# A second space for transposed tokens, DMA transposes spread over two stages, and W2's second half in pieces

## The chip, the cores and the metric

One core of one Trainium2 chip (trn2). The metric is the device time of one execution in microseconds (us), where lower is better. A profile is one execution taken by the hardware profiler; its span is some 1.8 us shorter than the timed run. The median of the kernel before moved by 3 us between sessions, so kernels of different sessions are best compared by their ratio to it.

## The reference, cut to what matters

```python
x = A_x                                                    # 2048 tokens x 1024, bf16
x = x + spectral(layernorm(x))                             # 2-D FFT filter, "layer A"
x = x + mish(layernorm(x) @ w1 + b1) @ w2                  # F = 3584, "layer B", dense
x = x + spectral(layernorm(x))
x = x + mish(layernorm(x) @ w1 + b1) @ w2
```

Only layer B is touched. It occurs twice ("layer one" and "layer two" below).

## The kernel before: what the change and the argument touch

The 2048 tokens are 16 tiles of 128 (`j`), or four chunks of 512 (`c`). A pair of chunks goes through the first matmul together: a Strassen-Winograd scheme takes seven block products of 4 matmuls each instead of eight. It needs sums of blocks of the tokens (made by VectorE) and sums of blocks of the weights (made by GpSimd in layer one, stored, and loaded ready-made in layer two). A "step" below is one pass of `quads`: 28 matmuls, 6.05 us. "Direct products" are those of the first matmul without the scheme.

```python
def fill_slot(self, b, fg):                 # weights of one step into one slot
    r = self.r_w1d[fg]
    if r.writes:                            # layer two: raw weights and sums come from DRAM
        self.dma(self.sp, b.ap, self.w1s_d[fg], ...)
        return
    self.load_w1(b.raw, fg, [b.res])        # 512 KB, sync queue
    for dst, x, y, op in (...):             # four sums on GpSimd
        self.op(self.pool, lambda e, ...: e.tensor_tensor(dst, x, y, op), reads=[b.res], writes=[b.rs])
    self.dma(self.pool, self.w1s_d[fg], b.ap, ...)          # stored for later, 896 KB

def turned(c, t, xn):                       # a tile transposed by eight DMAs, all on the sync queue
    x = XT[c % 2]                           # chunks 2 and 3 reuse the space of chunks 0 and 1
    for db in range(8):
        self.dma(sp, x.ap[:, db, t*P:(t+1)*P], xn.ap[:, db*P:(db+1)*P], ..., transpose=True)

# layer B, second half of the first pair, cut
early = self.open_slots("WE", self.ob["W2"], 3)
for n in range(3):
    self.fill_slot(early[n], 6 + n)
...                                         # direct first matmul of chunk 1, residual additions
ws = self.open_slots("WS", self.ob["WS"], 3)
for n in range(3):
    self.fill_slot(ws[n], 9 + n)
order = early + [ws[n % 3] for n in range(5)]
def after(n):                               # called when step n's products are issued
    if n in (3, 4):
        self.fill_slot(order[n + 3], 9 + n)
    if 2 <= n < 6:
        for i in range(2*n - 4, min(2*n - 2, 7)): load_w2(0, i)
quads(list(range(6, 14)), order, open_pair(), after)        # first block stage: 8 steps
...
for t in range(8): self.stats_dve(8 + t)                    # tiles 8 to 15, only now
self.scales(8, 8)
for n in range(16):                                         # second matmul of the first pair
    if n < 8:
        turned(2 + n // 4, n % 4, self.apply(8 + n))        # normalise and transpose
    mm2(n % 8 // 4, n % 4, n // 8)
    if n == 12: B = open_pair()                             # token sums of the second pair
quads(list(range(14)), order, B, after)                     # second block stage: 14 steps
```

A buffer allocated over another inherits all its readers and writers, so whoever is recorded as a reader of a tile makes the next writer of that space wait.

## Time and profile before

| | before |
|---|---|
| median of the runs beside the change | 1019.0 us (1016.8 to 1020.0) |
| profiled span, granted TensorE clock | 1014.7 us, 0.980 |
| layer one: approach (from the start of a group of 71 or 72 direct products, here at 137.12 us, to the first block product) | 41.44 us |
| layer one: first block stage, second block stage | 50.11, 108.77 us |
| layer two: the same three | 34.97, 49.30, 92.02 us |

The lines behind these numbers are in the prediction below. The kernel is bound by TensorE, so read its timeline: each row is a start, a length, a group of matmuls, and in brackets the hole before it with what ended the hole. Layer two is the same program without GpSimd's weight sums, and so it shows what layer one could be.

### The profile page before, as it was taken

The page shows a single profiled execution, that of the slowest core. Times are in us where ns is not written, and L with a number is a line of the kernel's source. Part 1 is how long each engine was busy: PE and PEld are TensorE (multiplying, and loading weights), DVE is VectorE, ACT ScalarE, POOL GpSimd, SP SyncE. Part 2 cuts the span into 40 slices and gives each one's busy share as a digit, 9 for nine tenths or more (in the row PEclk, how much of TensorE's full clock was granted, in tenths as well). Part 3 has the DMA queues.
Part 4 walks back from the last instruction along what each step waited for, and adds up shares of the span by engine and source line. Part 5 has one row for each costly group of instructions (what it writes and reads, how often), then busy time and mean ns, then how long its engine had stood idle before and what let it go on. Part 6 is the DMA issues. An engine that isn't in the chain of part 4 may idle for free. (4 is left out here: it accounts for less than half of the span.)

```text
span 1014.7 us, 13594 instructions
## 1 busy us (share of the span) xinstructions
PE 925.4 (91%) x5572; PEld 489.6 (48%) x5650; DVE 508.5 (50%) x915; ACT 377.6 (37%) x531; POOL 156.5 (15%) x184
## 2 busy tenths in 40 slices
PE   1799789999998499999998987999999989999998
PEld 0576565444443144444446765754444434444443
DVE  6797576558341655524335865655731145551111
ACT  7798473550000055510007975745300015550000
POOL 4831035342300060000431200000000000000000
PEclk9999899999999599999999998999999999999999
DMA  9969833467321054340751796233551124424000
GB/s 284 288 190 323 215 102 141 145 218 238 109 58 46 34 207 148 107 171 29 202 115 27 222 224 174 110 109 123 193 176 26 25 96 149 160 91 145 32 27 25
DMA packets 143598, 139.62 MB, mean 138 GB/s; under 512 B 74464, under 2 KB 124464, under 8 KB 143536
## 3 DMA queue, kind: packets, MB, share of 16 engines
q1 hardware_dynamic: 130432, 98.41, 32.6%
q0 software_dynamic: 10928, 38.69, 11.7%
q10 hardware_dynamic: 2176, 1.66, 0.5%
q8 instruction: 44, 0.72, 0.3%
q14 instruction: 18, 0.15, 0.0%
HBM read 100.64 MB, written 33.55 MB: 132 GB/s over the span
## 5 line engine op out<-in xcount | busy, mean ns | idle before, releaser
L1228 PE MATMUL PS<-ARENA 128*128 128x512 bf16 x1756 | 385.6, 379 | 1.9
L1177 PE MATMUL PS<-ARENA 128*128 128x512 f16 (+1 forms) x1210 | 274.1, 386 | 26.6 <-DVE ARENA L1156 12.6
L1228 PEld LDWEIGHTS PS<-ARENA 128*128 128x128 bf16 x1792 | 175.2, 98 | 211.8 <-DVE ARENA L1182 0.8
L1182 DVE TENSOR_TENSOR ARENA<-PS,ARENA 128x512 f32<-128x512 f32 x220 | 152.2, 692 | 116.7 <-PE PS L1177 115.1
L1177 PEld LDWEIGHTS PS<-ARENA 128*128 128x128 bf16 x1232 | 121.1, 99 | 178.9 <-DVE ARENA L1182 16.3
L1240 DVE TENSOR_TENSOR XS<-PS,XS 128x512 bf16<-128x512 f32 x63 | 43.3, 690 | 228.5 <-PE PS L1228 228.5
L577 ACT ACTIVATE ARENA<-PS 128x512 f32<-128x512 f32 (+2 forms) x66 | 51.8, 785 | 257.2 <-PE PS L1177 246.3
L1187 ACT ACTIVATE ARENA<-ARENA,B 128x512 bf16<-128x512 f32 x132 | 95.2, 721 | 61.4 <-DVE ARENA L1182 55.2
L1141 PE MATMUL PS<-ARENA 128*128 128x256 bf16 (+1 forms) x570 | 88.0, 311 | 0.4
L1084 POOL TENSOR_TENSOR ARENA<-ARENA 128x512 bf16<-128x512 bf16 x56 | 66.6, 1189 | 119.6 <-DMA ARENA<-in_B_w_dram 95.0
L1141 PEld LDWEIGHTS PS<-ARENA 128*128 128x128 bf16 x576 | 55.8, 99 | 27.7 <-issue 2.1
L469 DVE BATCH_NORM_STATS2 BN<-XS 128x6 f32<-128x512 bf16 x99 | 63.8, 673 | 5.3 <-DMA XS<-in_A_x_dram 4.3
L1145 ACT ACTIVATE ARENA<-PS,B 128x256 bf16<-128x256 f32 (+1 forms) x72 | 38.4, 542 | 41.8 <-PE PS L1141 41.2
L1156 DVE TENSOR_TENSOR ARENA<-ARENA 128x2048 f16<-128x2048 bf16 x16 | 19.8, 1238 | 60.0 <-DMA ARENA<-ARENA 41.3
L1187 ACT ACTIVATE ARENA<-PS,B 128x512 bf16<-128x512 f32 x44 | 30.3, 688 | 36.2 <-PE PS L1177 36.2
L441 ACT ACTIVATE RS<-MV,EPS 128x2 f32<-128x2 f32 (+2 forms) x5 | 1.5, 298 | 95.7 <-DVE MV L472 83.7
L802 PE MATMUL PS<-ARENA 128*128 128x256 bf16 x256 | 32.4, 273 | 3.8 <-DVE ARENA L791 3.2
L780 ACT ACTIVATE ARENA<-PS 128x1024 bf16<-128x1024 f32 x32 | 33.3, 1071 | 4.5 <-PE PS L776 4.5
L728 PE MATMUL PS<-FD,ARENA 128*128 128x256 bf16 (+1 forms) x256 | 31.8, 271 | 2.5 <-DVE ARENA L995 1.3
L784 DVE TENSOR_TENSOR ARENA<-ARENA 128x1024 bf16<-128x1024 bf16 x32 | 22.0, 689 | 19.8 <-ACT ARENA L780 14.2
L813 ACT ACTIVATE ARENA<-PS 128x1024 bf16<-128x1024 f32 x28 | 29.9, 1090 | 3.7 <-PE PS L802 3.7
L1023 PE MATMUL PS<-MT,ARENA 128*128 128x32 bf16 (+1 forms) x512 | 21.7, 200 | 10.3 <-DMA ARENA<-u_scratch 7.0
(95 smaller groups left out, 695.6 us busy)
## 6 DMA issues: line engine op xcount, KB each, us to landing
ARENA<-in_B_w_dram SPq DMA_DIRECT2D x68, 512.0 KB, 6.5
ARENA<-w1s_scratch SPq DMA_DIRECT2D x30, 896.0 KB, 4.6
w1s_scratch<-ARENA POOLq DMA_DIRECT2D x14, 896.0 KB, 4.3
u_scratch<-ARENA SPq DMA_DIRECT2D x14, 512.0 KB, 3.5
ARENA<-u_scratch SPq DMA_DIRECT2D x14, 512.0 KB, 6.1
w_scratch<-ARENA POOLq DMA_DIRECT2D x8, 512.0 KB, 7.6
ARENA<-w_scratch POOLq DMA_DIRECT2D x8, 512.0 KB, 5.5
out_dram<-XS SPq DMA_DIRECT2D x16, 256.0 KB, 2.0
```

Source lines behind the costliest of these rows:

```text
L469: self.op(self.dve, lambda e: e.bn_stats(self.BN[:, j, 6 * h:6 * h + 6], self.XS[:, j, 512 * h:512 * h + 512]), reads=[self.r_xs[j]], part ...
L577: fn = (lambda e: e.activation(dst, src, ACT.Copy)) if scale is None else \
L780: self.op(act, lambda e: e.activation(x.ap.rearrange("p a b -> p (a b)"), ps, ACT.Copy, scale=SIG), reads=banks, writes=[x.res])
L802: fns.append(lambda e, c=c, part=part: e.matmul(ps[:, c * 256:(c + 1) * 256], yk.ap[:, part, c * P:(c + 1) * P], t[:, (128, 0)[part]:(384, ...
L1084: self.op(self.pool, lambda e, dst=A(dst), x=A(x), y=A(y), op=op: e.tensor_tensor(dst, x, y, op), reads=[b.res], writes=[b.rs])
L1141: fns.append(lambda e, db=db, bank=bank, fl=fl: e.matmul(PS[:, bank, 0:w], wb.ap[:, db, fl * P:(fl + 1) * P], x.ap[:, db, tok], start=(db ...
L1145: self.op(act, lambda e, bank=bank, ft=ft: e.activation(at.ap[:, ft, tok], PS[:, bank, 0:w], ACT.Mish, bias=self.B1[:, ft:ft + 1]), reads= ...
L1177: self.group([lambda e, db=db: e.matmul(PS[:, bank, :], A[:, db, :], mov[:, db, :], start=(start and db == 0), stop=(db == 3), skip_group_ ...
L1182: self.op(dve, lambda e: e.tensor_tensor(dst.ap, PS[:, bank, :], x.ap, ALU.add), reads=[self.r_bank[bank], x.res], writes=[dst.res])
L1187: self.op(act, lambda e: e.activation(at.ap[:, ft, :], src, ACT.Mish, bias=self.B1[:, ft:ft + 1]), reads=[res, self.r_b1], writes=[ra])
L1228: fns.append(lambda e, i=i, ft=ft: e.matmul(PS[:, bank, :], at.ap[:, ft, t * P:(t + 1) * P], W2[h][ft // 4].ap[:, ft % 4, :], start=(i == ...
L1240: self.op(dve, lambda e: e.tensor_tensor(xs, PS[:, bank, :], xs, ALU.add), reads=[self.r_bank[bank]], writes=[self.r_xs[j]])
```

## The change

The intent: the second pair's transposes should no longer wait for the first pair's products, so that the token sums are there when the second block stage starts. So chunks 2 and 3 get spaces of their own; W2's second half moves into pieces of free space; statistics, normalisation and transposes of tiles 8 to 11 come forward into the first block stage; and GpSimd's first weight sums wait until the eighth tile (`xn[7]`) is normalised. Core of the diff:

```diff
-        self.ob = dict(AT0=0, AT1=36 * K, XT1=28 * K, XT0=120 * K, W2=64 * K, ...
+        self.ob = dict(AT0=0, AT1=36 * K, XT1=28 * K, XT0=120 * K, XT2=104 * K, XT3=112 * K, W2=64 * K, ..., XN2=140 * K,
@@ fill_slot
-    def fill_slot(self, b, fg):
+    def fill_slot(self, b, fg, after=()):
-            self.op(self.pool, ..., reads=[b.res], writes=[b.rs])
+            self.op(self.pool, ..., reads=[b.res] + list(after), writes=[b.rs])
@@ turned: queue closures instead of issuing; turn(n) issues the next n
+        def turn(n):
+            for _ in range(min(n, len(turning))):
+                turning.pop(0)()
@@ load_w2
-            W2[h][i] = self.alloc(f"W2_{h}_{i}", self.ob["W2"] + h * 28672 + i * 4096, [4, 512])
+            off = (28, 32, 120, 124, 92, 96, 100)[i] * 1024 if h else self.ob["W2"] + i * 4096
+            if h and not i and W2[1][0]:
+                off = 104 * 1024
@@ before the first block stage
-            self.fill_slot(early[n], 6 + n)
+            self.fill_slot(early[n], 6 + n, [xn[7].res])
...
+            if fg < 4:
+                for j in range(4 * fg, 4 * fg + 4):
+                    residual(j)
+            if fg == 3:
+                token_sums(0, last=False)
+            if fg == 4:
+                for j in range(8, 12):
+                    self.stats_dve(j)
+        self.scales(8, 4)
+        normal(8)
+        turn(8)
         ws = self.open_slots("WS", self.ob["WS"], 3)
         for n in range(3):
             self.fill_slot(ws[n], 9 + n)
+        B = token_sums(0)
@@ after(n) of the first block stage
+            if n < 3:
+                normal(9 + n)
+            elif n < 7:
+                self.stats_dve(9 + n)
+            turn(4)
@@ second matmul
+            if n == 0:
+                self.scales(12, 4)
+            if n < 4:
+                normal(12 + n)
             mm2(t // 4, t % 4, n // 8)
-            if n == 12:
-                B = open_pair()
+            turn(4)
+            if n == 10:
+                token_sums(1, last=False)
+                B = token_sums(1)
@@ after the second block stage
-        for i in range(7):
+        for i in (0, 4, 5, 6):
             load_w2(1, i)
```

The last lines are a side effect: three pieces of W2's second half stay where they are and aren't loaded again, six loads of 512 KB less in the whole kernel.

More of the change, by code (lines that the diff above doesn't have):

```diff
@@ L369, in layout @@
                       FT=140 * K, BT=144 * K + 512, WT=self.W1_OFF)
-        self.ob = dict(AT0=0, AT1=36 * K, XT1=28 * K, XT0=120 * K, W2=64 * K, JUNK=54 * K, SUMS=92 * K, TS=128 * K,
+        self.ob = dict(AT0=0, AT1=36 * K, XT1=28 * K, XT0=120 * K, XT2=104 * K, XT3=112 * K, W2=64 * K, JUNK=54 * K, SUMS=92 * K, TS=128 * K, XN2=140 * K,
                        WS=self.arena_bytes - 21 * K)
@@ L1083, in fill_slot @@
                               ("S4", "A12", "S2", ALU.subtract)):
-            self.op(self.pool, lambda e, dst=A(dst), x=A(x), y=A(y), op=op: e.tensor_tensor(dst, x, y, op), reads=[b.res],
+            self.op(self.pool, lambda e, dst=A(dst), x=A(x), y=A(y), op=op: e.tensor_tensor(dst, x, y, op), reads=[b.res] + list(after),
                     writes=[b.rs])
@@ L1091, in layer_B, with open_xt @@
         base = 28 * li
-        XT, AT, r_xt, r_at = [None, None], [None, None], [None, None], [None, None]
+        XT, AT, r_xt, r_at = [None] * 4, [None, None], [None] * 4, [None, None]
         nt, nh, no = [0], [0], [0]
+        def open_xt(c):
+            off = self.ob[f"XT{c}"]
+            XT[c] = self.alloc(f"XT{c}", off, [8, 512])
+            r_xt[c] = self.sub_res(XT[c], f"xt{c}h", 2, off, 8192)
+            for r in r_xt[c]:
+                r.begin()
         def transposed(c, t, xn, eng=None):
@@ L1099, in transposed @@
             if t == 0:
-                if XT[c % 2] is None:
-                    off = self.ob[f"XT{c % 2}"]
-                    XT[c % 2] = self.alloc(f"XT{c % 2}", off, [8, 512])
-                    r_xt[c % 2] = self.sub_res(XT[c % 2], f"xt{c % 2}h", 2, off, 8192)
-                for r in r_xt[c % 2]:
-                    r.begin()
+                open_xt(c)
             fns = []
@@ L1110, in transposed, with one @@
             self.group(fns, reads=[xn.res, self.r_ident], writes=[self.r_bank[bank]])
-            dst = XT[c % 2].ap[:, :, t * P:(t + 1) * P]
+            dst = XT[c].ap[:, :, t * P:(t + 1) * P]
             src = PSb[:, bank, :].rearrange("p (a b) -> p a b", b=P)
             fn = (lambda e: e.activation(dst, src, ACT.Copy)) if eng is act else (lambda e: e.tensor_copy(dst, src))
-            self.op(eng or dve, fn, reads=[self.r_bank[bank]], parts=[r_xt[c % 2][t // 2]])
+            self.op(eng or dve, fn, reads=[self.r_bank[bank]], parts=[r_xt[c][t // 2]])
+        turning = []
         def turned(c, t, xn):
-            xn.unread = False
-            x = XT[c % 2]
-            if t == 0:
-                for r in r_xt[c % 2]:
-                    r.begin()
-            for db in range(8):
-                self.dma(sp, x.ap[:, db, t * P:(t + 1) * P], xn.ap[:, db * P:(db + 1) * P], f"xt{c % 2}_{t}", reads=[xn.res],
-                         parts=[r_xt[c % 2][t // 2]], transpose=True)
+            x, r = XT[c], r_xt[c][t // 2]
+            for db in range(8):
+                def one(db=db):
+                    self.dma(sp, x.ap[:, db, t * P:(t + 1) * P], xn.ap[:, db * P:(db + 1) * P], f"xt{c}_{t}", reads=[xn.res],
+                             parts=[r], transpose=True)
+                    if db == 7:
+                        xn.unread = False
+                turning.append(one)
+        def turn(n):
+            for _ in range(min(n, len(turning))):
+                turning.pop(0)()
         def mm1(c, fg, half=None, mid=()):
             wb = self.w1_buf[fg]
-            x = XT[c % 2]
+            x = XT[c]
             tok = slice(0, 512) if half is None else slice(256 * half, 256 * half + 256)
@@ L1142, in mm1 @@
                         PS[:, bank, 0:w], wb.ap[:, db, fl * P:(fl + 1) * P], x.ap[:, db, tok], start=(db == 0), stop=(db == 7)))
-                self.group(fns, reads=[wb.res] + (r_xt[c % 2] if half is None else [r_xt[c % 2][half]]), writes=[self.r_bank[bank]])
+                self.group(fns, reads=[wb.res] + (r_xt[c] if half is None else [r_xt[c][half]]), writes=[self.r_bank[bank]])
                 at, ra = AT[c % 2], r_at[c % 2][ft]
@@ L1147, in mm1, with token_sums @@
                         reads=[self.r_bank[bank], self.r_b1], writes=[ra])
-        def open_pair():
-            T = [self.alloc(f"TS{i}", self.ob["TS"] + 4096 * i, [4, 512], F16) for i in range(3)]
-            lo, hi = [[XT[c].ap[:, 4 * k:4 * k + 4, :] for c in range(2)] for k in range(2)]
+        def token_sums(p, last=True):
+            c0, c1 = 2 * p, 2 * p + 1
+            lo, hi = [[XT[c].ap[:, 4 * k:4 * k + 4, :] for c in (c0, c1)] for k in range(2)]
             t3 = lo[1].bitcast(F16)
-            both = r_xt[0] + r_xt[1]
+            both = r_xt[c0] + r_xt[c1]
             tt = lambda dst, x, y, reads, writes: self.op(
                 dve, lambda e: e.tensor_tensor(dst, x, y, ALU.subtract), reads=reads, writes=writes)
+            if last:
+                tt(t3, hi[1], lo[1], r_xt[c0], r_xt[c1])
+                T = self.T
+                return {"B11": (lo[0], r_xt[c0]), "B21": (hi[0], r_xt[c0]), "B22": (hi[1], r_xt[c1]), "T3": (t3, r_xt[c1]),
+                        "T1": (T[0].ap, [T[0].res]), "T2": (T[1].ap, [T[1].res]), "T4": (T[2].ap, [T[2].res])}
+            self.T = T = [self.alloc(f"TS{i}", self.ob["TS"] + 4096 * i, [4, 512], F16) for i in range(3)]
             tt(T[0].ap, lo[1], lo[0], both, [T[0].res])
@@ L1159, in open_pair @@
             tt(T[2].ap, hi[0], T[1].ap, both + [T[1].res], [T[2].res])
-            tt(t3, hi[1], lo[1], r_xt[0], r_xt[1])
-            return {"B11": (lo[0], r_xt[0]), "B21": (hi[0], r_xt[0]), "B22": (hi[1], r_xt[1]), "T3": (t3, r_xt[1]),
-                    "T1": (T[0].ap, [T[0].res]), "T2": (T[1].ap, [T[1].res]), "T4": (T[2].ap, [T[2].res])}
         def open_sums():
@@ L1227, in mm2 @@
             for i, ft in enumerate(range(NF)):
-                fns.append(lambda e, i=i, ft=ft: e.matmul(
-                    PS[:, bank, :], at.ap[:, ft, t * P:(t + 1) * P], W2[h][ft // 4].ap[:, ft % 4, :],
+                fns.append(lambda e, i=i, ft=ft, w=W2[h][ft // 4]: e.matmul(
+                    PS[:, bank, :], at.ap[:, ft, t * P:(t + 1) * P], w.ap[:, ft % 4, :],
                     start=(i == 0), stop=(i == NF - 1 and not summed)))
@@ L1258, in load_w2 @@
         def load_w2(h, i):
-            W2[h][i] = self.alloc(f"W2_{h}_{i}", self.ob["W2"] + h * 28672 + i * 4096, [4, 512])
+            off = (28, 32, 120, 124, 92, 96, 100)[i] * 1024 if h else self.ob["W2"] + i * 4096
+            if h and not i and W2[1][0]:
+                off = 104 * 1024
+            W2[h][i] = self.alloc(f"W2_{h}_{i}", off, [4, 512])
             self.dma(sp, W2[h][i].ap, w2v[:, 4 * i:4 * i + 4, h * 512:(h + 1) * 512], f"w2_{h}_{i}", writes=[W2[h][i].res])
@@ L1346, in layer_B, with normal @@
             mm1(1, fg, 1)
+        def normal(j):
+            if j % 4 == 0:
+                open_xt(j // 4)
+            turned(j // 4, j % 4, self.apply(j))
         for fg in range(2, 6):
             mm1(1, fg)
-            for j in (2 * fg + 4, 2 * fg + 5):
-                residual(j)
+            if fg < 4:
[6 more added lines that the diff above has]
+                    self.stats_dve(j)
+        self.xn_buf = self.xn_out + [self.alloc(f"XN{i}", self.ob["XN2"] + i * 2048, [self.D]) for i in range(2)]
+        self.scales(8, 4)
+        normal(8)
+        turn(8)
         ws = self.open_slots("WS", self.ob["WS"], 3)
@@ L1361, in after @@
                     load_w2(0, i)
-        quads(list(range(6, 14)), order, open_pair(), after)
+            if n < 3:
[3 more added lines that the diff above has]
+            turn(4)
+        quads(list(range(6, 14)), order, B, after)
         for i in range(7):
@@ L1367, in layer_B @@
             self.fill_slot(order[n], n)
-        self.xn_buf = [self.alloc(f"XN{i}", self.ob["TS"] + i * 2048, [self.D]) for i in range(6)]
-        for t in range(8):
-            self.stats_dve(8 + t)
-        self.scales(8, 8)
+        self.xn_buf = [self.alloc(f"XN{i}", self.ob["TS"] + i * 2048, [self.D]) for i in range(4)]
         for n in range(16):
-            if n < 8:
-                b = self.apply(8 + n)
-                turned(2 + n // 4, n % 4, b)
+            if n == 0:
+                self.scales(12, 4)
+            if n < 4:
+                normal(12 + n)
             t = n % 8
             mm2(t // 4, t % 4, n // 8)
-            if n == 12:
-                B = open_pair()
+            turn(4)
+            if n == 10:
+                token_sums(1, last=False)
+                B = token_sums(1)
+        assert not turning
         def after(n):
```

## The prediction

> **What bounds the kernel now.** I read the page first (busy shares, the forty slices), then the waits of TensorE, then the timeline of TensorE, VectorE and the sync queue around each wait, then one table of windows. The kernel has two spectral layers and two dense layers; only the dense ones (from about 120 and from about 620 us) are touched.
>
> ```profile
> PE 925.4 (91%) x5572; PEld 489.6 (48%) x5650; DVE 508.5 (50%) x915; ACT 377.6 (37%) x531; POOL 156.5 (15%) x184
> PE   1799789999998499999998987999999989999998
> PEclk9999899999999599999999998999999999999999
> ...
> PE PS L1177 <- DVE ARENA L1156: 12.6, 2, 8.8
> PE PS L1177 <- DVE ARENA L1182: 11.8, 6, 8.1
> PE PS L1108 <- DVE ARENA L521: 5.2, 5, 3.4
> ```
>
> TensorE is busy 91% of the span, so only its holes matter. The fourteenth slice (330 to 355 us) falls to 4 tenths and its clock to 5 tenths: that is the hole in which the first dense layer waits for the token sums (L1156) of its second chunk pair. The waits list (total, times, longest) puts 12.6 us on those sums over both layers and 11.8 us on additions (L1182) that queue behind other VectorE work. The timeline shows the chain:
>
> ```profile
> 325.36 1.03 PE L1177 MATMUL PS<-ARENA 128*128 128x512 bf16 x4
> 335.15 5.30 PE L1177 MATMUL PS<-ARENA 128*128 128x512 f16 x12 [8.77 <-DVE ARENA L1156]
> 348.55 15.84 PE L1177 MATMUL PS<-ARENA 128*128 128x512 f16 x59 [8.09 <-DVE ARENA L1182]
> ...
> 332.61 5.00 DVE L1156 TENSOR_TENSOR ARENA<-ARENA 128x2048 f16<-128x2048 bf16 x4 [21.66 <-DMA ARENA<-ARENA]
> ...
> 243.73 87.67 SPq L250 DMA_TRANSPOSE ARENA<-ARENA  x64
> ```
>
> The 64 DMA transposes leave one queue one after the other (median 1.23 us each in the rows of that line, 1.37 with stalls), from 243.7 to 331.4 us. They start late because they write over the first pair's tokens, so they must wait for the first block products. The second products are due at 325.4, the sums start at 332.6 and take 5.0 us, and three tiles' worth of postponed residual and normalisation work then holds the adds until 348.6. In the second layer the same stretch has holes of 3.87 and 0.59 us.
>
> The table of windows compares the same work in both layers: approach to the first block products, first products, second products. Columns: window, its length, busy time of PE, PEld, DVE, ACT, POOL, clock, DMA share.
>
> ```profile
> 137.12:178.56 41.44, 36.96 (x242) 22.41 (x243) 29.50 (x48) 19.43 (x35) 24.39 (x23) 0.96 0.46 152
> 641.62:676.59 34.97, 34.75 (x242) 22.06 (x242) 21.25 (x48) 19.43 (x35) 0.00 (x0) 1.00 0.42 153
> 178.56:228.67 50.11, 48.48 (x222) 21.73 (x224) 28.41 (x40) 26.68 (x39) 18.77 (x18) 1.00 0.53 179
> 676.59:725.89 49.30, 48.30 (x221) 21.83 (x224) 28.17 (x40) 26.79 (x39) 0.00 (x0) 1.00 0.34 116
> 325.36:434.13 108.77, 90.44 (x386) 39.04 (x392) 61.88 (x103) 46.45 (x69) 17.15 (x18) 0.91 0.33 117
> 822.59:914.61 92.02, 86.41 (x386) 38.32 (x392) 54.35 (x76) 46.77 (x69) 0.00 (x0) 0.98 0.38 134
> ```
>
> First row against second: equal matmuls, but 6.47 us longer in layer one, where GpSimd works 24.39 us beside VectorE and in layer two not at all.
>
> **What the Trainium skill says.** "TensorE: Matmul & The Clock Gate", the part on the HAM clock gate: after an idle window of some 3.4 us the array runs at half clock until it has been busy again. The trace agrees: after the 8.77 us hole 12 matmuls took 5.30 us (0.44 each, against 0.216), after the 8.09 us hole 59 took 15.84, some 3.1 us too long. "SBUF — State Buffer", section "Who interferes with whom": VectorE and GpSimd share a port pair under an exclusive lock; VectorE copies and tensor_scalar in 2-port modes, and anything with two SBUF inputs, can be blocked by a GpSimd operation. The trace agrees: the normalisation (L521) takes 0.55 us alone and up to 1.28 beside GpSimd. "DMA: Bandwidth & Descriptors", section "Issuing engines are not separate DMA queues": the sequencer's issue time is usually small beside the transfer. Here it is not: 1.23 us of queue per transpose against 2.4 us to landing, so the queue is the resource to count.
>
> **The change, part by part.** (1) Tokens 8 to 15 get a space of their own (XT2, XT3), W2's second half moves into pieces of dead space. Half the transposes now go out during the first block products: 8 before them, 4 after each of the first six; the other 32 in the first eight groups of the second matmul. Those 32 take 32 x 1.23 = 39.4 us, starting once the queue has pushed the weight loads (some 14 us into the stage, as now), so they end about 54 us into a stage of 96.8 us; the sums are placed after the eleventh group, at 66.5. Hence the L1156 wait goes in both layers. Layer two's second stretch: 92.02 - 3.87 - 0.59 - 1.7 (12 cold matmuls, 4.33 - 12 x 0.216) = 85.9. Layer one should reach the same plus some 1.0 for the last tile's chain on VectorE (0.69 + 0.69 + 0.21 + six small operations + 0.55, 3.4 us, ahead of the first add): 86.9 against 108.77. **Gain 21.9 + 6.1.**
>
> (2) GpSimd's first twelve weight sums (16.4 us from first to last, 141.4 to 157.8) now wait for the eighth tile's normalisation. That frees VectorE where TensorE waited 3.38 and 0.67 us plus cold matmuls: layer one's approach should become layer two's 34.97. **Gain 6.5**, quads starting at about 172.1.
>
> (3) The price, in layer one. GpSimd now starts at 152.6 (layer two's time of that normalisation, 657.06, minus the offset of 504.5) and ends at 152.6 + 16.4 + about 2 of blocking = 171. VectorE meanwhile has eight residual additions (4.90 us alone, some 0.75 more each beside GpSimd) and the first token sum, to about 167. The second sum's space covers the buffer of the eighth normalised tile, which the GpSimd sums now count as reading, so it should wait for the last of them: 171.2. Then two sums 2.5, four tiles' statistics 5.53, scales 1.6, one normalisation 0.55, last sum 1.25, one add 0.69: 183.4. TensorE needs sum and add at the fifth product, 172.1 + 16 x 0.216 = 175.6. **Loss 7.8 plus some 3 of cold clock.**
>
> (4) The queue. Eight transposes (9.9 us) stand ahead of three weight loads: 181.4 + 9.9 + 0.4 issue + 3.8 to landing (as at 164.9 to 168.7 now) + 4.9 of GpSimd = 200.4. Step four of the delayed products needs them at 172.1 + 18.2 + 10.8 = 201.1: just hidden. Later steps carry at most 4 x 1.23 + 1.4 us of queue per 6.05 us step; I add **0.6 of loss** for the seventh slot, which already stands 0.63 us now. Layer two has no GpSimd sums: its normalisation ends near 675.5, before the products, loads land near 690 and are needed at 694.7, so nothing is lost.
>
> Sum: 21.9 + 6.1 + 6.5 - 7.8 - 3 - 0.6 = 23.1; 1019.6 - 23.1 = **996.5 us**, which I round to 996.
>
> **Rivals.** (A) Part 3 is avoided: the sums don't collide, or VectorE is ahead of the products as in layer two. For it: layer two's timeline leaves the last sum where TensorE wants it. Against: layer one's GpSimd work merely moves onto VectorE's busiest stretch. Then the loss is only the load path of part 4, some 2 us with the start at 172.6, and the time about 987. (B) Contention is worse, or transposes in the queue delay weight loads in steps 4 to 8: each transposed batch then takes over 6.05 us (1.37 each plus loads is already 6.9), slots come late by several us and the clock falls again: 1002 to 1005. (C) The sums at the eleventh group find transposes unfinished, so the wait merely moves: against it the 12 us of slack; it would give back 5 to 10 us, about 1003. (D) The transfers were hidden anyway: the waits list speaks against it, 8.8 and 8.1 us of it on TensorE's own path.
>
> **Range and chances.** The gains are firm (sizes known from the other layer); the loss in layer one is an estimate from four contended operations, 2 to 14 us. So 987 to 1005. The 2% line is 999.2, some 3 us above the figure: faster 0.70, same 0.29, slower 0.01.
>
> **What would show it.** Right: no wait of L1177 on L1156 near the second products, transposes in two groups, one ending before the second matmul and one half-way through it, the approach window near 35 us with no L1108 wait of 3 us. Part 3 right: a TensorE hole of 5 to 11 us within the first step of layer one's block products, released by VectorE, and the second token sum starting when GpSimd's twelfth sum ends. Part 4: that layer's fourth step free of a wait on GpSimd longer than 2 us. Wrong: a first block stage in layer one of 50 us (then rival A) or over 65 us, or a wait on transposes left in either layer.

## The result, and the profile after

The changed kernel took **1006.3 us** (median of four runs, 1005.8 to 1006.7) against 1019.0 before. The ratio is 0.9878, interval 0.9860 to 0.9895: 1.2% faster. I had said 996, and 1005 as the upper end of the range. (A ratio is the mean time of one kernel's runs over that of the other's runs of the same rounds, so it isn't quite the ratio of the medians quoted.)

First the page of the changed kernel, with the busy share and the clock in 40 slices of 25.1 us. The fourteenth slice, 4 tenths before, is full now. But the eighth to tenth (176 to 251 us) have fallen to 6, 7 and 8 tenths, and the clock there to 7, 9 and 8.

```profile
PE 928.6 (92%) x5650; PEld 490.0 (49%) x5650; DVE 509.1 (51%) x931; ACT 377.6 (38%) x531; POOL 157.7 (16%) x184
PE   1799699678999999999998997999999999999998
PEclk9999799798999999999999998999999999999999
```

Next TensorE's timeline in layer one, from the first block product on:

```profile
173.76 3.87 PE L1188 MATMUL PS<-ARENA 128*128 128x512 bf16 x16
185.66 15.21 PE L1188 MATMUL PS<-ARENA 128*128 128x512 f16 x60 [8.02 <-DVE ARENA L1193]
204.22 19.66 PE L1188 MATMUL PS<-ARENA 128*128 128x512 bf16 x84 [3.35 <-POOL ARENA L1084]
228.40 15.16 PE L1188 MATMUL PS<-ARENA 128*128 128x512 bf16 x56 [4.53 <-POOL ARENA L1084]
...
342.77 3.62 PE L1188 MATMUL PS<-ARENA 128*128 128x512 bf16 x16
347.16 13.12 PE L1188 MATMUL PS<-ARENA 128*128 128x512 f16 x60 [0.77 <-DVE ARENA L1193]
```

The holes at the second block stage (8.77 and 8.09 us) are gone; 0.77 is left. But the first block stage, which had only one of 0.63 us, now has three: 8.02 us in its first step, 3.35 before its fourth, 4.53 before its seventh. The same windows as before (length; busy time of PE, PEld, DVE, ACT, POOL; clock; DMA share; GB/s):

```profile
138.79:173.76 34.97, 34.91 (x244) 22.04 (x242) 27.87 (x47) 19.41 (x35) 17.81 (x14) 1.00 0.29 99
637.85:672.82 34.97, 34.91 (x245) 22.06 (x242) 28.58 (x69) 19.41 (x35) 0.00 (x0) 1.00 0.21 79
173.76:246.08 72.32, 55.56 (x226) 23.10 (x225) 44.57 (x78) 26.47 (x39) 26.49 (x26) 0.86 0.58 178
672.82:722.43 49.61, 48.69 (x225) 21.74 (x224) 35.12 (x55) 26.68 (x39) 0.00 (x0) 1.00 0.60 188
819.13:904.78 85.65, 84.86 (x393) 38.16 (x392) 48.41 (x70) 46.76 (x69) 0.00 (x0) 1.00 0.38 128
342.77:430.51 87.74, 85.38 (x393) 37.90 (x391) 50.84 (x79) 46.55 (x69) 16.04 (x16) 1.00 0.41 143
```

So layer one's approach fell from 41.44 to 34.97 us, its second block stage from 108.77 to 87.74, and layer two's from 92.02 to 85.65. That makes 33.9 us of gain. Layer one's first block stage rose from 50.11 to 72.32 and gave 22.2 of them back. Small differences elsewhere (mostly 1.7 us before the first approach) bring the two spans to 9.8 us apart. The second dense layer lost next to nothing: its first stage took 49.61 against 49.30.

What lies behind the three holes is in the rows of VectorE (L1298 residual additions, L1164 token sums, L521 normalisation, L1193 adds), of GpSimd (L1084 weight sums) and of the sync queue (L250 transposes, L251 loads):

```profile
156.31 12.85 DVE L1298 TENSOR_TENSOR XS<-XS,ARENA 128x1024 bf16<-128x1024 bf16 x8
169.08 2.17 DVE L1164 TENSOR_TENSOR ARENA<-ARENA 128x2048 f16<-128x2048 bf16 x1
173.59 2.49 DVE L1164 TENSOR_TENSOR ARENA<-ARENA 128x2048 f16<-128x2048 bf16 x2 [2.35 <-POOL ARENA L1084]
183.32 0.55 DVE L521 TENSOR_SCALAR FD<-XS,MV,RS 128x1024 bf16<-128x1024 bf16 x1
184.91 0.68 DVE L1193 TENSOR_TENSOR ARENA<-PS,ARENA 128x512 f32<-128x512 f32 x1
```

```profile
167.43 6.06 POOL L1084 TENSOR_TENSOR ARENA<-ARENA 128x512 bf16<-128x512 bf16 x4
199.23 4.93 POOL L1084 TENSOR_TENSOR ARENA<-ARENA 128x512 bf16<-128x512 bf16 x4 [24.89 <-PE PS L1188]
223.51 4.83 POOL L1084 TENSOR_TENSOR ARENA<-ARENA 128x512 bf16<-128x512 bf16 x4 [7.01 <-DMA ARENA<-in_B_w_dram]
```

```profile
183.89 11.03 SPq L250 DMA_TRANSPOSE ARENA<-FD  x8
194.97 2.29 SPq L251 DMA_DIRECT2D ARENA<-in_B_w_dram  x3
```

Beside GpSimd the eight residual additions took 12.85 us; before, without it, they took 4.90. The second token sum waited 2.35 us for GpSimd's twelfth sum, which ended at 173.49. So the add that TensorE needs in its first step came at 185.6 and not near 178: the first hole. The eight transposes that wait for the normalisation at 183.3 stood ahead of the weight loads in the sync queue, and those were therefore issued only from 194.97 on. GpSimd's sums for the fourth step then ended at 204.16, and TensorE resumed at 204.22: the second hole. The weights for the seventh step were issued at 216.77 and summed from 223.51 on: the third.

### The profile page after: what moved, and what is told of

The parts are those of the page before. It is cut to its first block, busy times and chain, and to the rows that moved or that the text cites.

```text
span 1004.9 us, 13677 instructions
## 1 busy us (share of the span) xinstructions
PE 928.6 (92%) x5650; PEld 490.0 (49%) x5650; DVE 509.1 (51%) x931; ACT 377.6 (38%) x531; POOL 157.7 (16%) x184
## 5 line engine op out<-in xcount | busy, mean ns | idle before, releaser
L1239 PEld LDWEIGHTS PS<-ARENA 128*128 128x128 bf16 x1792 | 175.2, 98 | 211.8 <-DVE ARENA L1193 0.8
L1193 DVE TENSOR_TENSOR ARENA<-PS,ARENA 128x512 f32<-128x512 f32 x220 | 152.1, 691 | 115.3 <-PE PS L1188 113.7
L1188 PEld LDWEIGHTS PS<-ARENA 128*128 128x128 bf16 x1232 | 121.1, 99 | 174.1 <-DVE ARENA L1193 15.9
L1084 POOL TENSOR_TENSOR ARENA<-ARENA 128x512 bf16<-128x512 bf16 x56 | 67.7, 1209 | 132.8 <-DVE ARENA L521 60.5
L1149 PEld LDWEIGHTS PS<-ARENA 128*128 128x128 bf16 x576 | 55.8, 99 | 26.8 <-DVE ARENA L1115 0.7
L1023 PE MATMUL PS<-MT,ARENA 128*128 128x32 bf16 (+1 forms) x512 | 22.0, 202 | 11.1 <-DMA ARENA<-u_scratch 7.7
L802 PEld LDWEIGHTS PS<-ARENA 128*128 128x128 bf16 x256 | 24.0, 98 | 11.9 <-DVE ARENA L791 5.6
```

The source lines that it names most:

```text
L802: fns.append(lambda e, c=c, part=part: e.matmul(ps[:, c * 256:(c + 1) * 256], yk.ap[:, part, c * P:(c + 1) * P], t[:, (128, 0)[part]:(384, ...
L1084: self.op(self.pool, lambda e, dst=A(dst), x=A(x), y=A(y), op=op: e.tensor_tensor(dst, x, y, op), reads=[b.res] + list(after), writes=[b.rs])
L1149: fns.append(lambda e, db=db, bank=bank, fl=fl: e.matmul(PS[:, bank, 0:w], wb.ap[:, db, fl * P:(fl + 1) * P], x.ap[:, db, tok], start=(db ...
L1188: self.group([lambda e, db=db: e.matmul(PS[:, bank, :], A[:, db, :], mov[:, db, :], start=(start and db == 0), stop=(db == 3), skip_group_ ...
L1193: self.op(dve, lambda e: e.tensor_tensor(dst.ap, PS[:, bank, :], x.ap, ALU.add), reads=[self.r_bank[bank], x.res], writes=[dst.res])
L1239: fns.append(lambda e, i=i, ft=ft, w=W2[h][ft // 4]: e.matmul(PS[:, bank, :], at.ap[:, ft, t * P:(t + 1) * P], w.ap[:, ft % 4, :], start=( ...
```

## The experiments

Each ran three rounds beside the kernel before; the columns of this overview are TensorE's windows and holes in layer one, read from each timeline. The holes stand before the rest of step 1, before step 4, 7 and 8 of the first block stage.

| kernel | median us | ratio | approach | first stage | holes 1 / 4 / 7 / 8 |
|---|---|---|---|---|---|
| before | 1016.7 to 1019.7 | 1 | 41.44 | 50.11 | 0 / 0 / 0.63 / 0 |
| changed | 1006.3 | 0.9878 | 34.97 | 72.32 | 8.02 / 3.35 / 4.53 / 0 |
| e1_no_gate | 1001.4 | 0.9844 | 41.52 | 60.06 | 0 / 2.64 / 4.36 / 0 |
| e2_no_false_dep | 1005.1 | 0.9889 | 34.97 | 71.99 | 7.63 / 3.11 / 5.71 / 0 |
| e3_loads_first | 1004.3 | 0.9875 | 34.97 | 70.81 | 14.76 / 0 / 3.17 / 0 |
| e4_few_turns | 1003.1 | 0.9863 | 34.97 | 69.86 | 8.02 / 3.55 / 1.57 / 3.72 |
| e5_gate_alone | 1012.7 | 0.9950 | 34.97 | 52.90 | 2.02 / 0 / 0.97 / 0 |
| e7_nogate_loads | 998.1 | 0.9805 | 41.38 | 57.49 | 0.44 / 0 / 5.03 / 0.56 |
| e8_staged | 992.4 | 0.9747 | 34.97 | 59.43 | 0 / 0 / 8.61 / 0 |
| e9_staged_few | 985.7 | 0.9684 | 34.97 | 52.33 | 0 / 0 / 2.32 / 0.36 |
| e10_pool_fill | 1002.0 | 0.9827 | 34.97 | 66.56 | 0 / 0 / 7.37 / 4.56 |
| e11_few_pool | 997.6 | 0.9789 | 34.97 | 65.39 | 0 / 0 / 6.96 / 4.14 |
| e12_staged_w2 | 995.6 | 0.9760 | 34.97 | 62.42 | 0 / 0 / 10.84 / 0 |
| e13_few_w2 | 993.5 | 0.9742 | 34.97 | 61.65 | 0 / 0 / 9.53 / 0 |
| e14_no_turns | 990.2 | 0.9716 | 34.97 | 51.86 | 0 / 0 / 2.38 / 0 |
| e15_few_w2late | 984.9 | 0.9674 | 34.97 | 50.86 | 0 / 0 / 1.38 / 0 |
| e16_w2late | 1004.6 | 0.9867 | 34.97 | 71.78 | 8.02 / 3.39 / 4.38 / 0 |

### Without the wait on the eighth tile

```diff
-            self.fill_slot(early[n], 6 + n, [xn[7].res])
+            self.fill_slot(early[n], 6 + n)
```

> The changed kernel without the wait of GpSimd's first weight sums on the eighth normalised tile, all else kept. My theory (hole chain in layer one: late GpSimd work delays VectorE, VectorE delays the first transposes, these delay weight loads): the approach window of layer one goes back from 34.97 to about 41.4 us, but the first block stage falls from 72.3 to about 53 us, as the last token sum is ready before it is needed and the queue is about on time: the 8.0 us hole gone, the 3.35 and 4.53 us holes each near 1 us. Net about 13 us faster than the changed kernel: 993 to 998. Rival 1 (the transposes slow the weight loads in the DMA engines or the queue wherever they stand): the 3 to 5 us holes stay, 1001 to 1003. Rival 2 (the wait is a good part of the change): slower than 1006.

Measured: 1001.4 us. The approach went back to 41.52 us and the first hole vanished, as the theory said. The other two stayed, which rival 1 had said:

```profile
181.53 16.57 PE L1188 MATMUL PS<-ARENA 128*128 128x512 bf16 x76
200.74 19.99 PE L1188 MATMUL PS<-ARENA 128*128 128x512 bf16 x84 [2.64 <-POOL ARENA L1084]
225.08 13.98 PE L1188 MATMUL PS<-ARENA 128*128 128x512 bf16 x56 [4.36 <-POOL ARENA L1084]
```

The sixteen products of the first step run straight on. So the wait on the eighth tile is worth 6.5 us in the approach and costs the whole first hole; within the changed kernel it is a net loss of 5 us by the medians, 3.5 by the ratios. But the later holes don't come from it.

### The same wait, without recording a reader

GpSimd waits for the tile's writer as before but isn't marked as a reader, so the second token sum needn't wait for it. No data hazard is involved, since GpSimd never reads the tile.

```diff
+        gate = [w for r in after for w in r.wait_r()]
-            self.op(self.pool, ..., reads=[b.res] + list(after), writes=[b.rs])
+            t = self.pool.add(..., waits=gate + b.res.wait_r() + b.rs.wait_w())
+            self.mark(self.pool, t, [b.res], [b.rs])
```

> The changed kernel, GpSimd's sums still waiting for the eighth normalised tile but no longer recorded as readers of it, so the second token sum needn't wait for the twelfth GpSimd sum. My theory: the 2.35 us wait of VectorE goes, the 8.0 us hole becomes about 5.7 us, the later holes stay, as the weight loads and TensorE come earlier together: about 1004. Rival (the false reader is the main cause of the hole): hole below 2 us, 998. Rival (contention takes its place, as two more sums then run beside GpSimd): hole about 7 us, 1005.5.

Measured: first hole 7.63 us, not 5.7. The last rival was right: the 2.35 us wait went, but the three token sums now ran beside GpSimd's last four operations and took 6.35 us together instead of 3.74, while those four took 6.92 instead of 6.06.

```profile
168.49 6.35 DVE L1166 TENSOR_TENSOR ARENA<-ARENA 128x2048 f16<-128x2048 bf16 x3
```

The false reader is real, but it costs only 0.4 us of the hole. What costs is GpSimd work beside VectorE's two-input additions, whether it meets the residual additions or the token sums.

### Weight loads ahead of the first eight transposes

```diff
         normal(8)
-        turn(8)
         ws = self.open_slots("WS", self.ob["WS"], 3)
         for n in range(3):
             self.fill_slot(ws[n], 9 + n)
+        turn(8)
```

> The changed kernel with the three weight loads of the second slot set ahead of the first eight transposes in the queue. My theory: the 3.35 us hole before the fourth step goes, since these loads land some 15 us earlier; but GpSimd then sums them beside VectorE's eight small scale operations and the normalisation, which costs VectorE some 4 us, so the first hole grows to about 12 us; the third stays. Net 1003 to 1006. Rival (small operations are not held up, or GpSimd is done in time): first hole stays at 8, second goes with its cold clock, 1001.

Measured: 1004.3 us, as expected. The hole before step 4 is gone, which shows that its cause is these eight transposes in front of the loads. The first hole grew to 14.76 us, because GpSimd now summed the second three slots from 174.2 on, beside VectorE's small scale operations: between the end of the statistics (182.38) and the normalisation lie 5.7 us, where it was 1.6. The normalisation itself took 1.44 us instead of 0.55, and the last token sum 2.17 instead of 1.22; only the statistics kept their 1.23 to 1.27 us beside GpSimd:

```profile
188.06 1.44 DVE L521 TENSOR_SCALAR FD<-XS,MV,RS 128x1024 bf16<-128x1024 bf16 x1
```

One hole was traded for another, and the time hardly moved.

### Two transposes per step

```diff
-            turn(4)            # after(n) of the first block stage
+            turn(2)
...
-            turn(4)            # second matmul
-            if n == 10:
+            turn(6)
+            if n == 12:        # token sums of the second pair
```

> The changed kernel with two transposes after each block product in place of four, six per group of the second matmul in place of four, and the second pair's token sums after the thirteenth group in place of the eleventh. My theory: holes of 8.0 and 3.35 us stay, the 4.53 us hole before the seventh step (weights issued 4.6 us late behind transposes) falls below 1 us, and with it the cold clock after it; the later transposes still end before the sums: about 1000. Rival (the load itself is slowed in flight by the two W2 loads beside it, 6.7 us to landing): hole 2.5 us or more, 1003 or above.

Measured: 1003.1 us. The hole before step 7 shrank to 1.57 us, but one of 3.72 opened before step 8. Neither side was right: the order in the queue matters, but the load for step 8, issued at 219.10, reached GpSimd only at 228.28. (My expectation called the load in the changed kernel 4.6 us late. By a better reckoning below it was some 1.5.)

### The wait alone, on the kernel before

```diff
-            self.fill_slot(early[n], 6 + n)
+            self.fill_slot(early[n], 6 + n, [xn[7].res])
```

> The kernel before with one part of the change alone: GpSimd's first weight sums wait for the eighth normalised tile. My theory: the approach window of layer one falls from 41.4 to 35.0 us; the late GpSimd work delays residual additions and token sums, but without the four tiles' statistics in front of the last sum VectorE is done some 2 us after TensorE needs it, and the weight loads stand ahead of no transposes: first block stage 52 to 54 us in place of 50.1. Net 3 to 4 us faster than before. Rival (the wait alone brings the 8 us hole): first stage 58 us or more, no gain or a loss.

Measured: 1012.7 us, ratio 0.9950 (0.9924 to 0.9975). Approach 34.97 us, first stage 52.90, first hole 2.02: the sizes expected. Here VectorE has no statistics of four more tiles before the last token sum, and no loads wait behind transposes. So the wait is a small gain by itself. It became a loss through the work that the other parts of the change put behind it.

### Both blamed orders undone, the spread kept

The edits of the first and the third experiment together.

> The changed kernel without the wait on the eighth tile and with the three weight loads ahead of the first transposes: both parts that the runs so far blame are undone, the transposes themselves stay spread as in the change. My theory: approach 41.5 us, no hole before the fourth step; a first hole of about 2 us, as GpSimd's second three slots run beside the small scale operations; a hole of about 2 us before the seventh step, since the engines of the DMA now have the weight loads and stores behind them when W2 comes. First block stage about 55 us, 994 to 997. Rival (the transposes alone crowd the queue): holes before the seventh and eighth step of 4 us or more, 999 or above.

Measured: 998.1 us, above the 994 to 997 that I expected; first hole 0.44, none before step 4, but 5.03 us before step 7, where I had expected about 2: the rival's number for the hole. The spread transposes by themselves leave a late step 7.

### GpSimd released slot by slot

The wait stays, but only the first slot takes it. The second is released by the third token sum and the third by the ninth normalised tile. Loads stand ahead of the transposes, and no reader is recorded.

```diff
-        for n in range(3):
-            self.fill_slot(early[n], 6 + n, [xn[7].res])
+        self.fill_slot(early[0], 6, [xn[7].res])
...
                 token_sums(0, last=False)
+                self.fill_slot(early[1], 7, [self.T[2].res])
...
-        normal(8)
-        turn(8)
+        self.fill_slot(early[2], 8, [normal(8).res])
         ...                                   # three fill_slot(ws[n])
+        turn(8)
```

> The changed kernel with GpSimd's three first slots released one by one: the first by the eighth normalised tile, the second by the third token sum, the third by the ninth normalised tile, without recording GpSimd as a reader, and the weight loads ahead of the first transposes. My theory (the cost is GpSimd work beside VectorE's two-input additions and small operations, and a late queue): approach 35 us, first hole below 2 us, none before the fourth step, one of 1 to 4 us before the seventh: first block stage 51 to 56 us, 985 to 990. Rival (GpSimd now runs out of time): holes before steps two to six, stage above 60 us.

Measured: 992.4 us, a first stage of 59.43: both above what I expected. The first two holes are gone with the approach still at 34.97 us, so the causes found for them were right, though this run removes them together. The third became larger than in any run before:

```profile
173.33 34.70 PE L1190 MATMUL PS<-ARENA 128*128 128x512 bf16 x157
216.64 13.59 PE L1190 MATMUL PS<-ARENA 128*128 128x512 bf16 x55 [8.61 <-POOL ARENA L1085]
```

The sync queue's load for step 7 and GpSimd's sums after it, in the same timeline:

```profile
205.57 1.58 SPq L251 DMA_DIRECT2D ARENA<-in_B_w_dram  x1
...
211.76 4.82 POOL L1085 TENSOR_TENSOR ARENA<-ARENA 128x512 bf16<-128x512 bf16 x4 [13.13 <-DMA ARENA<-in_B_w_dram]
```

The products run 34.7 us without a hole, so the queue has no time to catch up: four transposes per step and the loads take longer than a step (this load comes 8.0 us after the W2 loads of the step before, at 197.61). The load for step 7 was issued at 205.57. Its slot was free at about 199.4 (26.1 us after the first product, as in the kernel before, where the issue came at 204.65 after a start at 178.56).

### The same with two transposes per step

> The same with two transposes after each block product and six per group of the second matmul, sums after the thirteenth group. My theory: the hole before the seventh step falls below 1 us as its weights are issued on time, 983 to 988. Rival (bandwidth, not the queue's order, sets when these weights land): the same as with four transposes, within 1 us.

Measured: **985.7 us**, ratio 0.9684 (0.9668 to 0.9700). The hole fell to 2.32 us, not below 1, and the load was issued at 199.77, on time:

```profile
199.77 2.91 SPq L251 DMA_DIRECT2D ARENA<-in_B_w_dram  x3
210.69 6.22 PE L1190 MATMUL PS<-ARENA 128*128 128x512 bf16 x28 [2.32 <-POOL ARENA L1085]
```

So six of the 8.6 us were the order in the queue. The rest is not: the load took 6.0 us to reach GpSimd where it took 4.3 before.

### The two loads from GpSimd's queue

```diff
-                self.fill_slot(order[n + 3], 9 + n)
+                self.fill_slot(order[n + 3], 9 + n, q=pool)     # the weight load is issued by GpSimd
```

> The kernel with staged release (four transposes per step, 8.61 us hole before the seventh step) with only the weight loads of the seventh and eighth step issued from GpSimd's queue in place of the sync queue. In the staged kernel that load was issued 6.1 us after the step that frees its slot and took 6.2 us to land, against 4.3 in the kernel before. My theory (most of the hole is waiting behind transposes in the queue): issued on time from a queue without transposes, the hole falls to 2 to 3 us, time 985 to 987. Rival (the transposes and W2 loads hold the data up in the DMA engines, whichever queue it comes from): the hole stays at 6 us or more, 990 or above.

> The best kernel so far (staged release, two transposes per step) with the same two loads from GpSimd's queue. My theory: there the load is already issued on time, so nothing is gained from the order: within 1.5 us of 985.7, hole before the seventh step 1.5 to 3 us. Rival (queue order still costs): hole below 1 us, 983.

Measured: 1002.0 and 997.6 us. My theory fell. In both kernels the load was issued within 0.3 us of its time, but it took 10.8 and 10.4 us until GpSimd went on:

```profile
203.48 0.92 POOL L251 DMA_DIRECT2D ARENA<-in_B_w_dram  x1 [1.06 <-PE PS L1190]
214.30 4.83 POOL L1085 TENSOR_TENSOR ARENA<-ARENA 128x512 bf16<-128x512 bf16 x4 [9.90 <-DMA ARENA<-in_B_w_dram]
```

Three things differ there: a store of 896 KB, issued 1.6 us earlier, stands ahead on that queue, the W2 loads of the sync queue no longer wait behind this load, and GpSimd issues it instead of SyncE. No run tells which of them costs the 6 us. Taking the load off the busy queue didn't make it land earlier here.

### W2's first half earlier, later, and no transposes at all

```diff
             # e12, e13: W2 pieces 0 | 1, 2 | 3 to 6 after steps 1, 2, 3
             # e15, e16: W2 pieces 0 to 2 | 3, 4 | 5, 6 after steps 5, 6, 7
             # e14: turn() removed from after(n); turn(7) per group of the second matmul, sums at n == 14
```

> The best kernel so far (staged release, two transposes per step) with W2's first half loaded after the first three products in place of the third to sixth, so that no W2 load is in flight beside the weights of the seventh and eighth step. There this load was issued on time but landed after 6.0 us instead of 4.3, and from GpSimd's queue, with W2 in flight beside it, after 9.5. Theory formed from that (what is left of the hole is the DMA engines' load, not the queue): landing falls to 4 to 5 us, the 2.32 us hole to below 0.8, time 983 to 984.5. Rival (transposes in flight slow it whatever else moves): hole unchanged at 2 us or more, within 1 us of 985.7.

> The staged kernel with four transposes per step, W2's first half loaded after the first three products. Theory: here the queue is the limit; five more W2 issues of some 0.55 us now stand ahead of the seventh step's load, which is thus 8 to 9 us late instead of 6.1 and lands faster: the 8.61 us hole stays between 8 and 11 us, 991 to 995. Rival (bandwidth was the cause of that hole too): hole 5 us or less, 988 or below.

> The best kernel (staged release, loads first) with no transposes after the block products at all: eight before them, seven after each of the first eight groups of the second matmul, sums after the fifteenth group. If transposes cause the hole before the seventh step: load issued on time, landing back at 4.3 to 4.6 us, hole below 1 us (from 2.32). If W2 traffic causes it: landing stays near 6 us, hole 2 us. In either case the sums now come so late that the second products of layer one wait some 3 us, and they may wait for transposes: 984 to 989 in total; the holes decide, not the total.

> The best kernel (two transposes per step) with W2's first half loaded after the fifth to seventh step, that is behind the weights of the seventh step. If W2 in front of or beside that load causes the hole: landing 4.3 to 4.8 us, hole before the seventh step below 1 us, and 983 to 984.5, unless the eighth step's load, which now has W2 beside it, comes late by 1 us or so. If transposes cause it: hole stays at 2 us or more, about 985.7.

> The changed kernel with only W2's first half moved behind the fifth to seventh step. If W2 matters as much as the order in the queue: the seventh step's load has two W2 issues less before it (some 1.2 us) and nothing big in flight, so its 4.53 us hole falls to about 2 us; the 8.0 and 3.35 us holes stay. About 1002.5. If transposes alone matter: hole 3.5 us or more, 1005.

Measured: 993.5, 995.6, 990.2, 984.9 and 1004.6 us. For the first of them my theory was wrong: with W2 moved forward, two megabytes of it stood in front of the load, which was issued 5.6 us late again and landed late as well. The second came out as expected (hole 10.84; the time 0.6 us above the range). In the third, where the last transposes had left the queue 13.6 us before, the load was on time and the hole still 2.38 us, so W2 and stores beside it are enough for that. (Its total, above the range, also has a hole of 3.05 us in the second products.) In the fourth, without W2 in front or beside, it was 1.38 us: less, but not below 1. In the changed kernel itself (the fifth) moving W2 hardly changed the hole, 4.38 us. That is the number that I had set for "transposes alone matter", but not its proof: the load was now on time, and its way had grown from 6.74 to 8.08 us.

All these numbers fit one sum. The hole before step 7 should be the 0.63 us of the kernel before, plus the time by which the load is issued after its slot is free, plus the time by which its way to GpSimd's first sum exceeds 4.33 us:

| kernel | slot free | issued | late | to GpSimd | 0.63 + late + excess | hole measured |
|---|---|---|---|---|---|---|
| before | 204.65 | 204.65 | 0 | 4.33 | 0.63 | 0.63 |
| changed | 215.3 | 216.77 | 1.5 | 6.74 | 4.5 | 4.53 |
| e8_staged | 199.4 | 205.57 | 6.1 | 6.19 | 8.6 | 8.61 |
| e9_staged_few | 199.8 | 199.77 | 0 | 6.03 | 2.3 | 2.32 |
| e10_pool_fill | 203.2 | 203.48 | 0.3 | 10.82 | 7.4 | 7.37 |
| e12_staged_w2 | 200.2 | 210.26 | 10.1 | 4.48 | 10.9 | 10.84 |
| e13_few_w2 | 198.7 | 204.28 | 5.6 | 7.67 | 9.5 | 9.53 |
| e14_no_turns | 201.2 | 201.16 | 0 | 6.08 | 2.4 | 2.38 |
| e15_few_w2late | 200.1 | 200.06 | 0 | 5.08 | 1.4 | 1.38 |
| e16_w2late | 215.7 | 215.73 | 0 | 8.08 | 4.4 | 4.38 |

(The slot is free 26.1 us after the first product where no hole came before. In the two kernels with earlier holes I took the start of VectorE's last add of that step, which in the kernel before coincides with the issue.) The same sum gives the hole before step 7 within 0.05 us in the runs that are not in the table (e1 to e5, e7, e11). It is an accounting: it says how much was a late issue and how much a slow way, but not why. So in the changed kernel 1.5 us of the third hole were the queue's order and 2.4 us a slower way of the data.

**What stays open**: which companion slows the data by how much. The longest way of this load on the sync queue, 8.08 us, had no W2 beside it but four transposes and a store of 896 KB issued 0.6 us before; 4.48 us had four transposes and neither. That points at the stores, which the late slots put just there. All the traces agree: in the five kernels with no store issued in the 9 us before the load (before, e3, e5, e7, e12) the way took 4.17 to 4.90 us, in the ten with one 5.08 to 8.08. The closest pair is e7 and e8: in both the sync queue issued two W2 pieces, four transposes, this load and two more W2 pieces, but only e8 had a store near, 7.5 us before. Its way took 6.19 us, that of e7 4.17:

```profile
212.11 2.44 SPq L251 DMA_DIRECT2D ARENA<-in_B_w_dram  x3
216.28 4.83 POOL L1084 TENSOR_TENSOR ARENA<-ARENA 128x512 bf16<-128x512 bf16 x4 [26.48 <-PE PS L1188]
```

(The last row names a product as what ended GpSimd's wait, but the load landed 4.0 us after its issue, at 216.1, so it was the load.) So W2 loads and transposes beside the load are not enough for a slow way. But no run took a store away alone, and how much W2 adds to it stays open too.

e9_staged_few and e15_few_w2late are the fastest and not distinguishable from each other (0.9668 to 0.9700 and 0.9657 to 0.9691).

## Why the prediction was wrong

The direction was right and the mechanism mostly too; the time missed by 10 us. By its own steps:

- **Part 1, the second block stages: right.** Gains of 21.9 and 6.1 us were predicted, 21.0 and 6.4 measured. No wait on the token sums was left in either layer, and the sums began at 316.2, some 27 us before the stage. The runs bear the cause out: e5, without the new spaces, keeps both holes (8.00 and 8.62 us), and the kernels with them wait there for 0.77 us at most, except e14, whose sums come late by intent (3.05).
- **Part 2, the approach: right.** 6.5 us predicted, 6.47 measured, at exactly layer two's 34.97 us.
- **Part 3, the price in the first step: right in size.** A hole of 7.8 us was predicted, 8.02 measured. The cold clock after it was put at 3 us; 60 matmuls took 15.21 us where 12.95 are due (60 x 0.2158), so 2.3. The wait of the second token sum on GpSimd's twelfth sum was there. Its share was overrated: e2 shows that without it contention costs nearly as much. The residual additions took 12.85 us, not the 10.9 of the estimate. That this did no harm was luck: VectorE was done with them and the first sum at 171.2, but had to wait for GpSimd until 173.5 anyway. (A reading was low, too: a normalisation beside GpSimd took up to 1.46 us in the approach, not 1.28.)
- **Part 4, the queue: this is the step that failed, by size.** "Just hidden" had two numbers 0.7 us apart, 200.4 and 201.1, made of eight estimates. With the profile's later start of 1.7 us they are 202.1 and 202.8. Measured, the sums for step 4 were ready at 204.16, 2.1 us later, and TensorE at 200.87, 1.9 us earlier: a hole of 3.35 us. On the side of the sums grew the end of the normalisation (183.9 instead of 183.1), the eight transposes (11.1 us up to the first load instead of 10.3) and the way to GpSimd (4.26 instead of 3.8). On TensorE's side the 18.2 us were wrong: they count three whole steps, 84 matmuls, but `quads` issues the last 8 matmuls of a step behind the first 8 of the next, so step 4 is due after 76 (16 and 60 in the timeline), 1.7 us sooner. The "0.6 of loss" for the seventh slot became 4.53. I counted the queue's occupancy, and my own figure for a later step, 4 x 1.23 + 1.4 = 6.3 us, was already longer than the 6.05 us of a step; I put 6.9 us into a rival and neither into the sum. I took the load's way as that of the kernel before, where no store was near. Each hole also brought cold clock: 84 matmuls in 19.66 us (1.5 too long) and 56 in 15.16 (3.1 too long, small waits included). Together the stage lost 22.2 us instead of 11.4.
- **Rival B was nearer than the main line**: it named late slots and a second fall of the clock, with 1002 to 1005. Rival C and D did not occur. Rival A's statement that only the load path would be left without the collision is close to e7, although with the approach given back.
- **The miss in one sum.** 10.8 us are the first block stage (22.2 instead of 11.4), 0.6 part 1, and 1.9 the small differences elsewhere, mostly the profile's later start. Against these stands 3.1 us: the timed median from which I subtracted, 1019.6, was that much above the time of the profiled run, 1016.5, from which all terms came. 10.8 + 0.6 + 1.9 - 3.1 = 10.2, the distance between 996.5 and the profiled run, 1006.7.

Where did the gain go? It was not lost in the stage that the change aimed at. It was given back in layer one's first block stage, where three engines at once got new work: VectorE (statistics and normalisation ahead of the sum that TensorE needs), GpSimd (moved beside VectorE) and the sync queue (transposes ahead of loads). e8 and e9 show that orders alone recover some 13 and then 20 us of it (by the ratios), with the same work.

## What to carry to other kernels

When transfers are moved into an earlier stage, write down for every load of that stage the time at which its slot becomes free, what then stands in front of it in its queue, and what lands beside it; a margin smaller than the errors of the estimates behind it (here 0.7 us out of eight) doesn't count as hidden, so put a part of the possible loss into the sum. An engine that is moved out of one stage's way lands beside another engine's work: ask which of that engine's operations stand on the path, and release the work piece by piece instead of all at once. Put loads with a deadline ahead of transfers without one in the same queue, and spread the latter so thinly that the queue is empty when a slot becomes free.

## What the Trainium skill lacked or had wrong

- "SBUF — State Buffer", section "Who interferes with whom": VectorE's two-input additions and GpSimd do slow each other as it says, and it names a VectorE operation 6.8 times and a GpSimd operation 1.5 times slower for opposite orders of issue; but it has no figure for both issuing back to back. Here eight additions of 128x1024 bf16 with both inputs in SBUF took 12.85 us beside GpSimd instead of 4.90, and three token sums 6.35 instead of 3.74, while GpSimd's groups of four took 5.5 to 6.9 us instead of 4.85.
- "DMA: Bandwidth & Descriptors", section "Issuing engines are not separate DMA queues": the issue time "is usually small relative to the DMA itself". For DMA transposes of 128x128 it was not: 1.23 us of the queue against 2.4 us to landing (medians of the kernel before), and eight of them delayed the loads behind them by 11 us.
- The same page: no section gives the way of a 512 KB load under the traffic of other queues. From its issue to GpSimd's first sum step 7's load took 4.2 to 4.9 us on the sync queue with no store of 896 KB issued in the 9 us before it, 5.1 to 8.1 with one, and 10.4 and 10.8 from GpSimd's queue.
- "TensorE: Matmul & The Clock Gate", Part 1: an idle window of some 3.4 us is named. Here a hole of 2.64 us (e1) was already followed by slow matmuls (84 in 19.99 us, where 18.1 are due; granted clock 0.67 between 200.7 and 203.0 us), one of 2.32 us (e9) was not (28 in 6.22, where 6.04 are due), and neither was one of 3.55 us (e4, 84 in 18.30). That the window is free-running, as the page says, can account for the long hole that did no harm, but not for the short one that did: no wholly idle window of 3.4 us fits into 2.64. So a hole under 3.4 us is no guarantee.
